# First feed-forward layer in 64-row halves of the array, second layer behind the values (beacon attention and maxout FFN, one core)

## The chip, the cores and the metric

One core of one Trainium2 chip. The metric is the device time of one execution in microseconds (us). The kernel's inputs and its output are f32 in device memory; inside it works in bf16 with f32 accumulation.

## What is computed

Causal attention over 8 batches of 8 heads, 576 tokens of 64 elements each. In front of the keys stand 16 "beacon" keys that every token sees. The 64-element outputs of the 8 heads are laid side by side, which gives a matrix x of 4608 tokens by 512. A feed-forward network follows: three weight matrices of 512 by 768, of whose products the elementwise largest is kept, and an output matrix of 768 by 512.

```
scores = q @ k_all^T / 8, causal on the 576 keys, open on the 16 beacons
a      = exp(scores - max);  a /= sum(a)
x      = heads side by side of (a @ v_all)
h      = maximum(maximum(x @ w1, x @ w2), x @ w3)
out    = h @ w_out
```

## The kernel before

Scores are made transposed, keys on partitions. A pair of heads shares one 128-partition tile: head 0 on partitions 0 to 63, head 1 on 64 to 127, for queries (qT) and keys (kT). So a score matmul contracts over 64 rows, and the two heads' matmuls lie in the two row halves of the array (`emit_scores`, L498 to L521). For each pair there are four groups of such matmuls; each fills at most two PSUM banks, is passed through exp by ScalarE into at_sb (L524) and is then masked, mostly by GpSimd (L543).

`emit_pv` (L563) multiplies the probabilities with the values. Four heads (a "quad", two pairs) run at once in the four 32-column strips of the array; a batch has two quads, each in two halves of 288 queries. A first pass with a matrix of ones gives the sums. `invert_sums` (L598) takes the logarithm and exp(-log) on ScalarE, and `multiply` (L610) scales the results on VectorE into xT, a ring of four batches (L616).

The first layer of the network, `mm1_unit` (L635), uses the full array: for 512 tokens, 128 of the 768 columns and one weight matrix, four matmuls of 128 rows (the four 128-row pieces of the 512 inputs) into one bank, or two such units into two banks. VectorE then copies the bank into hT (first matrix, L654) or takes the maximum with what is there (L656). The first 512 tokens are done in pieces of 256 (`mm1_halves`, L658). The second layer, `mm2_unit` (L677), takes 128 tokens: six matmuls of 512 columns, a copy by VectorE (L694), a store (L720).

Inputs come in f32 by DMA into eight staging buffers (`load_pair`, `load_v`), are cast to bf16, mostly by GpSimd (L255, L311), and are turned, the early pairs by TensorE (L384, L393, L435), those from pair 14 on by a transposing DMA (`cross_piece`, L374). All loads, transposes and stores of the loop go through SP's queue in the order of the steps.

The order of the work on every engine is written out by hand: `first_steps` (to L1072, the first two batches and a part of the network) and `loop_steps` (L1073 to L1614). A step names a function of the table `steps` (L851) and its arguments: "scores" with pair and group, "values" with quad and half, "ffn 1" for one first-layer or second-layer unit, "ffn 2" for two at once, "load", "cast", "cross" and "store" for the movement of data. After the list, `emit_all` (L1616) does the last values and the rest of the network. PSUM has eight banks: two score tiles of two banks (sc), two single banks (pv0, pv1), and one more tile of two banks (wide).

Of the kernel before, what the change touches and what calls it, by code (L numbers as in the profile page):

```python
# [8 lines left out]
FP32 = mybir.dt.float32  # L9
# [7 lines left out]
def kernel(  # L17
# [24 lines left out]
    n_tokb = n_tokens // TOKB  # L42
    FH = d_ff // 2
# [19 lines left out]
    RING = 4  # L63
# [52 lines left out]
    ffn_h = ctx.enter_context(tc.tile_pool(name="ffn_h", bufs=2))  # L116
# [3 lines left out]
    sc_psum = ctx.enter_context(tc.tile_pool(name="sc_psum", bufs=2, space=PSUM))  # L120
    pv_psum = ctx.enter_context(tc.tile_pool(name="pv_psum", bufs=1, space=PSUM))
    ffn_stack = ctx.enter_context(ExitStack())
# [4 lines left out]
    xT = const.tile([128, n_ct, RING * S], BF16, name="xT")  # L127
    NB_PE = Nb * B_PE
# [40 lines left out]
    def single(n=512):  # L169
        i = at_single[0] % 2  # L170
        at_single[0] += 1
        return pv_bank(i, [128, n], FP32)

# [290 lines left out]
    def turn_pair(p, q_copy):  # L464
        ps = next_tile(BF16)
# [32 lines left out]
    def emit_scores(p, gi, idle=0, now=True):  # L498
# [4 lines left out]
        ps = next_tile()  # L503
# [14 lines left out]
        exp = L(emit_exp, p, gi, ps)  # L518
        if now:
            exp()  # L520
        return exp  # L521

    def emit_exp(p, gi, ps):
        nc.scalar.activation(  # L524
            out=both_heads(p, gi), in_=ps[:, :, 0 : g_width(p, gi)], func=AF.Exp, scale=scale
        )
# [34 lines left out]
    ready = [-1]  # L561

    def emit_pv(quad, hf, first=0, last=len(passes), banks=None):  # L563
        b, g = divmod(quad, n_quad)
        v_sb = v_tiles[b]
        for p in range(PPQ * quad, PPQ * (quad + 1)):
            assert all((p, gi) in masked for gi in range(1 if b == 0 and hf == 0 else NG))
# [28 lines left out]
    products = []  # L596

# [12 lines left out]
    def multiply(count=len(passes)):  # L610
        for _ in range(min(count, len(products))):
# [9 lines left out]
            if g == n_quad - 1 and n == len(passes) - 1:  # L621
                ready[0] = 2 * b + hf

    def finish_pv():
        invert_sums()
        multiply()
# [3 lines left out]
    hTs = {}  # L630
    MID = TOKB // 2

    alone = [False]

    def mm1_unit(tb, ft, i, ps):  # L635
        if tb not in hTs:
            hTs[tb] = ffn_h.tile([128, n_ft, TOKB], BF16, name="hT")
        two = len(ps.shape) == 3
        h = hTs[tb][:, ft : ft + 2] if two else hTs[tb][:, ft]
        c0 = tb * TOKB % (RING * S)  # L640
        n0 = min(TOKB, RING * S - c0)
        for f in range(1 + two):
            dst = ps[:, f] if two else ps
            for x0, o0, n in ((c0, 0, n0), (0, n0, TOKB - n0)):
                for ct in range(n_ct if n > 0 else 0):
                    nc.tensor.matmul(  # L646
                        dst[:, o0 : o0 + n],
                        w_in[i][:, ct, 128 * (ft + f) : 128 * (ft + f + 1)],
                        xT[:, ct, x0 : x0 + n],
                        start=(ct == 0),  # L650
                        stop=(ct == n_ct - 1),
                    )
        if i == 0:
            (by_act if alone[0] else by_dve)(h, ps)  # L654
# [3 lines left out]
    def mm1_halves(tb, ft, i, lo, hi, ps):  # L658
        if tb not in hTs:
            hTs[tb] = ffn_h.tile([128, n_ft, TOKB], BF16, name="hT")  # L660
        h = hTs[tb][:, ft : ft + 2, lo:hi]
        ps = ps.rearrange("d (f t) -> d f t", f=2)
        for f in range(2):
            for ct in range(n_ct):
# [3 lines left out]
                    xT[:, ct, tb * TOKB + lo : tb * TOKB + hi],  # L668
# [3 lines left out]
        if i == 0:  # L672
            by_dve(h, ps)
        else:
            nc.vector.tensor_max(h, h, ps)

    def mm2_unit(tb, tt, ps):  # L677
        hT = hTs[tb]
        two = len(ps.shape) == 3
        for t in range(tt, tt + 1 + two):  # L680
            for ft in range(n_ft):
                nc.tensor.matmul(  # L682
                    ps[:, t - tt] if two else ps,
                    hT[:, ft, 128 * t : 128 * (t + 1)],
# [4 lines left out]
        if y_pool:  # L689
            y = y_pool[0].tile([128, 2, d_model], FP32, name="y")  # L690
        else:
            y = early.tile([128, 1, d_model], FP32, name=f"y{len(y_out) % 2}")
        n = 1 + two
        nc.vector.tensor_copy(y[:, 0:n], ps if two else ps[:, None])  # L694
        y_out.append((tb * TOKB + 128 * tt, n, y))

    def mm2_last(tb, tt, cuts):
        hT = hTs[tb]
        c0 = tb * TOKB + 128 * tt
        y = y_pool[0].tile([128, 2, d_model], FP32, name="y")[:, 0]  # L700
        for i in range(len(cuts) - 1):
            lo, hi = cuts[i : i + 2]
            ps = single()[:, 0 : hi - lo]
            for ft in range(n_ft):
                nc.tensor.matmul(
                    ps,
                    hT[:, ft, 128 * tt : 128 * (tt + 1)],
# [5 lines left out]
            nc.sync.dma_start(out[c0 : c0 + 128, lo:hi], y[:, lo:hi])  # L713
# [10 lines left out]

    units = []
    for tb in range(n_tokb):
        need = 2 * ((TOKB * (tb + 1) - 1) // S) + 1
        if tb == 0:  # L730
            for n, lo in ((0, 0), (need, MID)):
                for i in range(3):
                    for ft in range(0, n_ft, 2):
                        units.append((n, mm1_halves, (tb, ft, i, lo, lo + MID)))
        for i in range(0 if tb else 3, 3):
            for ft in range(n_ft):
                units.append((need, mm1_unit, (tb, ft, i)))
        for tt in range(TOKB // 128):
# [931 lines left out]
```

## Time and profile before

| what | value |
|---|---|
| median of three runs | 290.21 us (288.81 to 291.39) |
| span of the profiled execution, first to last instruction | 287.1 us |
| instructions in the span | 8822 |
| mean granted TensorE clock | 0.997 |
| TensorE busy | 278.4 us |
| VectorE busy | 169.7 us |
| ScalarE busy | 143.8 us |
| GpSimd busy | 121.6 us |
| read and written in device memory | 35.13 MB, 9.44 MB |

For the profiled execution only its span is given. The three runs are 1.7 to 4.3 us longer than it.

How to read the lines that follow. In the groups of instructions a row is line, engine, operation, output<-inputs, shapes, xcount | busy us, mean ns of one | idle time before them and what ended it. In a timeline a row is start us, duration us from the first start to the last end of the merged instructions, engine, line, operation, shapes, count. A matmul's duration is a model that includes its way through the array; how fast matmuls follow each other is read from their starts. PE is TensorE, PEld its weight loads, DVE VectorE, ACT ScalarE, POOL GpSimd, SP the queue that issues most DMAs.

### The profile page before, as it was taken

Reading aid. Unit: us, or ns where it says so; the run is one execution under the profiler, and the core shown is the slowest. Engines: PE = TensorE matmul, PEld = TensorE weight load, DVE = VectorE, ACT = ScalarE, POOL = GpSimd, SP = SyncE. Lnnn points to the kernel's source line nnn. Section 1 sums busy time; section 2 is a strip of 40 time slices with the busy share of each in tenths; the row PEclk is TensorE's granted clock in tenths of the full one; section 3 lists DMA queues with packets and bytes.
Section 4 is the critical chain, followed back from the end, with each engine's and each line's share of the span. In section 5 each row is a group of like instructions: output and inputs, shape, how many; then the busy total and the mean of one; then the engine's idle time right before and its main releaser. Section 6 shows DMA issues by size and latency. Waiting matters only on the chain.

```text
span 287.1 us, 8822 instructions
## 1 busy us (share of the span) xinstructions
PE 278.4 (97%) x3706; PEld 160.2 (56%) x3731; DVE 169.7 (59%) x317; ACT 143.8 (50%) x242; POOL 121.6 (42%) x252
## 2 busy tenths in 40 slices
PE   8999999999999999999999999999999999999994
PEld 7656777754646454545456787445544545444442
DVE  2456878766575657465745755567466655373372
ACT  3876676835647564736483268444853452201200
POOL 4562327736484584737376446653633230000000
PEclk9999999999999999999999999999999999999998
DMA  8999998999999987999999989999983003002104
GB/s 154 174 166 209 222 245 158 244 204 211 191 158 159 172 118 134 195 176 184 184 229 191 194 170 221 222 168 177 189 323 123 2 2 148 0 0 107 41 0 147
DMA packets 118231, 45.30 MB, mean 158 GB/s; under 512 B 107312, under 2 KB 112944, under 8 KB 118192
## 3 DMA queue, kind: packets, MB, share of 16 engines
q1 hardware_dynamic: 111984, 39.20, 74.7%
q0 software_dynamic: 5648, 5.21, 11.8%
q8 instruction: 29, 0.48, 0.7%
q10 hardware_dynamic: 560, 0.33, 0.5%
q14 instruction: 10, 0.08, 0.1%
HBM read 35.13 MB, written 9.44 MB: 155 GB/s over the span
## 4 chain that ended last, share of the span: by engine, by line
PE 89%; ACT 3%; DMA 2%; DVE 2%; POOL 1%; issue 1%; ACTq 0%; POOLq 0%
PE pv L646 21%; PE sc L646 15%; PE wide L646 8%; PE pv L682 6%; PE sc L509 6%; PE sc L682 5%; PE wide L682 4%; PE pv L584 4%; PE wide L584 4%; PE sc L584 4%; DMA quad<-in_k_dram 2%; PE wide L509 2%; ACT at_sb L524 2%; PE pv L473 2%; PE sc L665 1%; PE pv L665 1%
## 5 line engine op out<-in xcount | busy, mean ns | idle before, releaser
L524 ACT ACTIVATE at_sb<-sc 128x736 bf16<-128x736 f32 (+5 forms) x95 | 79.4, 868 | 59.2 <-PE sc L509 58.6
L543 POOL TENSOR_SCALAR_AFFINE_SELECT at_sb<-at_sb 128x256 bf16<-128x256 bf16 (+2 forms) x143 | 52.4, 385 | 109.3 <-ACT at_sb L524 101.2
L646 PEld LDWEIGHTS <-w_sb 128*128 128x128 bf16 x648 | 61.1, 98 | 60.7 <-issue 4.9
L646 PE MATMUL pv<-xT,w_sb 128*128 128x512 bf16 (+1 forms) x315 | 65.3, 347 | 0.3
L646 PE MATMUL sc<-xT,w_sb 128*128 128x512 bf16 (+1 forms) x205 | 45.6, 363 | 0.7 <-issue 0.2
L656 DVE TENSOR_TENSOR hT<-hT,pv 128x512 bf16<-128x512 bf16 x48 | 32.4, 686 | 13.2 <-PE pv L646 13.2
L524 ACT ACTIVATE at_sb<-wide 128x736 bf16<-128x736 f32 (+3 forms) x33 | 27.7, 840 | 23.6 <-PE wide L509 23.5
L255 POOL CAST p<-st 96x768 bf16<-96x768 f32 x48 | 38.2, 825 | 0.0
L682 PEld LDWEIGHTS <-hT 128*128 128x128 bf16 x210 | 19.5, 98 | 23.5 <-issue 1.1
L616 DVE TENSOR_TENSOR xT<-pv,recip 128x288 bf16<-128x288 f32 (+2 forms) x48 | 14.2, 351 | 26.4 <-ACT recip L606 26.3
L509 PE MATMUL sc<-qT,kT 64*128 64x288 bf16 (+6 forms) x298 | 27.8, 277 | 1.6 <-DVE kT L443 0.7
L656 DVE TENSOR_TENSOR hT<-hT,sc 128x1024 bf16<-128x1024 bf16 (+1 forms) x19 | 20.8, 1104 | 12.6 <-PE sc L646 12.5
L509 PEld LDWEIGHTS <-kT 64*128 64x128 bf16 x400 | 14.6, 94 | 20.8 <-issue 13.0
L584 PEld LDWEIGHTS <-v_sb 128*32 128x32 bf16 (+1 forms) x1408 | 24.8, 96 | 1.7 <-issue 0.6
L646 PE MATMUL wide<-xT,w_sb 128*128 128x512 bf16 (+1 forms) x110 | 24.5, 364 | 0.1
L682 PE MATMUL pv<-w_out_sb,hT 128*128 128x512 bf16 x83 | 19.9, 380 | 0.1
L311 POOL CAST v_sb<-st 128x1536 bf16<-128x1536 f32 (+2 forms) x21 | 18.4, 897 | 0.0
L654 DVE CAST hT<-pv 128x512 bf16<-128x512 f32 x20 | 13.7, 688 | 5.0 <-PE pv L646 5.0
L682 PE MATMUL sc<-w_out_sb,hT 128*128 128x512 bf16 x68 | 16.3, 380 | 0.2
L665 PEld LDWEIGHTS <-w_sb 128*128 128x128 bf16 x144 | 13.0, 98 | 3.4 <-issue 1.4
L606 ACT ACTIVATE recip<-lnd 128x288 f32<-128x288 f32 x32 | 14.2, 443 | 1.0
L694 DVE COPY y<-pv 128x512 f32<-128x512 f32 x14 | 9.7, 692 | 8.4 <-PE pv L682 8.1
(119 smaller groups left out, 278.8 us busy)
## 6 DMA issues: line engine op xcount, KB each, us to landing
st<-in_q_dram SPq DMA_DIRECT2D x24, 288.0 KB, 5.2
st<-in_k_dram SPq DMA_DIRECT2D x24, 288.0 KB, 6.3
st<-in_v_dram SPq DMA_DIRECT2D x24, 256.0 KB, 5.5
out_dram<-y SPq DMA_DIRECT2D x9, 512.0 KB, 3.8
out_dram<-y SPq DMA_DIRECT2D x17, 256.0 KB, 4.1
w_sb<-in_moe_w_dram POOLq DMA_DIRECT2D x6, 384.0 KB, 8.7
st<-in_v_dram SPq DMA_DIRECT2D x8, 224.0 KB, 4.9
st<-in_v_dram SPq DMA_DIRECT2D x8, 160.0 KB, 4.8
```

What stands on the lines that cost most here:

```text
L255: cast(t16.rearrange("p r h d -> p h r d"), st[0:QP, i * NQ2 : (i + 1) * NQ2].rearrange("p (h r d) -> p h r d", h=2, r=QR),)
L311: cast(v_sb[0:n, t:t1].rearrange("p t h d -> p (t h d)"), st[0:n, (t - t_lo) * H * D : (t1 - t_lo) * H * D],)
L509: nc.tensor.matmul(ps[:, e, off : off + q1 - q0], kT[hs, 128 * t : 128 * t + 128], qT[hs, q0:q1], start=True, stop=True, tile_position=(64 ...
L524: nc.scalar.activation(out=both_heads(p, gi), in_=ps[:, :, 0 : g_width(p, gi)], func=AF.Exp, scale=scale)
L543: nc.gpsimd.affine_select(out=view, in_=view, compare_op=ALU.is_ge, fill=0.0, base=x0, pattern=[[0, 2], [1, hi - lo]], channel_multiplier=-1,)
L584: nc.tensor.matmul(ps[bank][32 * j : 32 * j + 32, lo + q0 - qa : lo + qb - qa], lhsT, at_view(PPQ * quad + j // 2, t, j % 2, q0, qb), star ...
L606: nc.scalar.activation(out=recip, in_=lnd, func=AF.Exp, scale=-1.0)
L616: nc.vector.tensor_mul(xT[:, 2 * g + part - 1, c0 + ca : c0 + cb], ps[bank][:, lo : lo + cb - ca], recip[:, ca:cb],)
L646: nc.tensor.matmul(dst[:, o0 : o0 + n], w_in[i][:, ct, 128 * (ft + f) : 128 * (ft + f + 1)], xT[:, ct, x0 : x0 + n], start=(ct == 0), stop ...
L656: nc.vector.tensor_max(h, h, ps)
L665: nc.tensor.matmul(ps[:, f], w_in[i][:, ct, 128 * (ft + f) : 128 * (ft + f + 1)], xT[:, ct, tb * TOKB + lo : tb * TOKB + hi], start=(ct == 0),
L682: nc.tensor.matmul(ps[:, t - tt] if two else ps, hT[:, ft, 128 * t : 128 * (t + 1)], w_out_sb[:, ft, :], start=(ft == 0), stop=(ft == n_ft ...
```

## The change

`first_steps` stays. From the loop's start on:

- First layer. A unit now takes two blocks of 288 tokens (the first time two of 320) and works in the two 64-row halves of the array, each with a block and a PSUM bank of its own. As a half of the array reads only its own 64 partitions, the other 64 rows of weights and of x are copied across: the weights once (wC, six copies on VectorE, step "cross w"), x for each batch (xC, four copies, nearly all on GpSimd, step "cross x"). A unit is 16 matmuls in eight pairs.
- PSUM. From the loop's start there are four tiles of two banks, and each step names the one it uses ("place").
- Order. Score groups and single units alternate. Each batch's second layer ("out", two tiles of 128 tokens, sometimes one) stands behind the values of the batch's second quad. The last units and the last second-layer tiles are now steps of the list as well.
- Buffers. xT holds three batches instead of four; hT is one ring of 1152 tokens; there are four output buffers instead of nine. Four casts at the loop's start move from GpSimd to ScalarE.

The new functions:

```diff
+    blocks = [(TOKB, (2 * S - TOKB) // 2)] + [(S * b, HALF) for b in range(2, B)]
...
+    def cross_w(i, e, copy):
+        copy(wC[i][own(e)], w_in[i][own(1 - e)])
+
+    def cross_x(k, g, e, copy):
+        t0, n = blocks[k]
+        t0 += e * n
...
+        c0 = t0 % (RING * S)
+        copy(
+            xC[k][own(e), 2 * g : 2 * g + 2, 0:n],
+            xT[own(1 - e), 2 * g : 2 * g + 2, c0 : c0 + n],
+        )
...
+    def mm1_next(place, by_i="dve"):
+        k, i, ft = units.pop(0)
...
+        ps = tile_at(place)[:, :, 0:n]
+        cols = slice(128 * ft, 128 * (ft + 1))
+        for ct in range(n_ct):
+            for w, over in ((w_in[i], False), (wC[i], True)):
+                for e in range(2):
+                    c0 = (t0 + e * n) % (RING * S)
+                    x = xC[k][own(e), ct, 0:n] if over else xT[own(e), ct, c0 : c0 + n]
+                    nc.tensor.matmul(
+                        ps[:, e],
+                        w[own(e), ct, cols],
+                        x,
+                        start=(ct == 0 and not over),
+                        stop=(ct == n_ct - 1 and over),
+                        tile_position=(64 * e, 0),
+                    )
+        c0 = t0 % (2 * S)
+        take(i, hT[:, ft, c0 : c0 + 2 * n].rearrange("d (e t) -> d e t", e=2), ps, by[by_i])
...
+    def mm2_next(n, place):
...
+        y = y_pool[0].tile([128, 2, d_model], FP32, name="y")
+        nc.vector.tensor_copy(y[:, 0:n], ps[:, 0:n])
```

The steps at the loop's start, up to the first unit and a little beyond (the last number of a step that uses PSUM is its place):

```diff
+        ("ffn", "pv", 1),
         ("late",),
...
+        ("cross x", 0, 0, 0, "pool"),
+        ("cross w", 0, 0, "dve"),
+        ("cross w", 0, 1, "dve"),
+        ("scores", 8, 0, 0, 3),
+        ("mask", 8, 0, "pool"),
+        ("scores", 8, 2, 0, 1),
+        ("mask", 8, 2, "pool"),
+        ("values", 3, 0, 0),
+        ("invert",),
+        ("values", 3, 1, 2),
+        ("multiply", 3),
+        ("invert",),
+        ("multiply", 3),
+        ("cross x", 0, 0, 1, "pool"),
+        ("cross x", 0, 1, 0, "pool"),
+        ("cross x", 0, 1, 1, "pool"),
+        ("cast", 10, "act", "act"),
+        ("load", 1),
+        ("cast", 11, "act", "act"),
+        ("load", 1),
+        ("cross w", 1, 0, "dve"),
+        ("out", 2, 3),
+        ("store", 1),
+        ("cross w", 1, 1, "dve"),
+        ("out", 2, 1),
+        ("store", 1),
+        ("pair", 10, "act", 0),
+        ("keys", 10, "act"),
+        ("pair", 11, "act", 2),
+        ("keys", 11, "act"),
+        ("scores", 8, 3, 0, 3),
+        ("mask", 8, 3, "pool"),
+        ("unit", 1),
...
+        ("scores", 8, 1, 0, 0),
         ("mask", 8, 1, "pool"),
...
+        ("unit", 2),
```

The end of a later batch, before and after:

```diff
-        ("values", 11, 0, "pv"),
-        ("invert",),
-        ("exp", 24, 2),
-        ("values", 11, 1, "ring"),
...
-        ("multiply",),
-        ("invert",),
-        ("multiply",),
-        ("ffn 2",),
-        ("cast", 28, "pool", "pool"),
-        ("ffn 1", "pv0"),
-        ("scores", 24, 3, 0),
-        ("scores", 25, 0, 0),
...
+        ("unit", 0),
+        ("values", 11, 0, 3),
+        ("invert",),
+        ("values", 11, 1, 1),
+        ("multiply", 3),
+        ("cross x", 4, 1, 0, "pool"),
+        ("invert",),
+        ("multiply", 3),
+        ("cross x", 4, 1, 1, "pool"),
+        ("cast", 28, "pool", "pool"),
+        ("load", 1),
+        ("out", 2, 2),
+        ("store", 1),
+        ("out", 2, 0),
+        ("store", 1),
+        ("scores", 24, 0, 0, 3),
+        ("mask", 24, 0, "pool"),
+        ("unit", 1),
```

More of the change, by code (lines that the diff above doesn't have):

```diff
@@ L620, in multiply, with take, mm1_halves @@
             )
[L621 to L630, printed above, removed]
[L631 to L652 removed]
+            if n == len(passes) - 1:
+                in_xT.add((quad, hf))
+    MID = TOKB // 2
+    def take(i, h, ps, by_i=None):
         if i == 0:
[L654 removed]
+            (by_i or by_dve)(h, ps)
         else:
             nc.vector.tensor_max(h, h, ps)
[L658 to L661, printed above, removed]
+    def mm1_halves(ft, i, lo, ps):
         ps = ps.rearrange("d (f t) -> d f t", f=2)
```

1078 lines of the change are left out of this document (532 added, 546 removed).

## The prediction

> **What bounds the kernel now.** I read the profile's page first (busy times, then the chain of work that ended last), then the table of stretches, then the timeline of single stretches.
>
> ```profile
> PE 278.4 (97%) x3706; PEld 160.2 (56%) x3731; DVE 169.7 (59%) x317; ACT 143.8 (50%) x242; POOL 121.6 (42%) x252
> PE 89%; ACT 3%; DMA 2%; DVE 2%; POOL 1%; issue 1%; ACTq 0%; POOLq 0%
> ```
> ```profile
> 0.00:55.20 55.20, 51.60 (x966) 38.66 (x967) 35.06 (x104) 37.75 (x62) 27.39 (x68) 1.00 1.08 196
> 55.20:283.40 228.20, 226.70 (x2742) 121.49 (x2766) 134.27 (x213) 106.04 (x180) 94.18 (x185) 1.00 0.84 149
> ```
>
> TensorE (PE) is busy 97% and is 89% of the chain. The second fence gives, for each stretch, its length and the busy time of PE, its weight loads, VectorE (DVE), ScalarE (ACT) and GpSimd (POOL). The changed list of steps begins at 55.2 us. From there to 283.4, PE is busy 226.7 of 228.2 us at granted clock 1.00. No other engine passes 59% of that stretch, so after 55.2 us only a change in PE's own time, or a new wait, can move the end.
>
> A busy PE is not a streaming PE, though. The next rows show where it pays without streaming: start, time from the first start to the last end, shape, count.
>
> ```profile
> 122.05 2.75 PE L682 MATMUL pv<-w_out_sb,hT 128*128 128x512 bf16 x12
> 124.64 1.03 PE L646 MATMUL pv<-xT,w_sb 128*128 128x512 bf16 x4
> ...
> 125.28 0.38 PE L646 MATMUL pv<-xT,w_sb 128*128 128x512 bf16 x1
> 125.60 0.32 PE L509 MATMUL sc<-qT,kT 64*128 64x336 bf16 x2
> ...
> 125.75 0.37 PE L509 MATMUL sc<-qT,kT 64*128 64x288 bf16 x4
> ...
> 125.87 0.25 PE L509 MATMUL sc<-qT,kT 64*128 64x208 bf16 x2
> 125.96 0.32 PE L509 MATMUL wide<-qT,kT 64*128 64x288 bf16 x4
> 126.22 0.39 PE L646 MATMUL pv<-xT,w_sb 128*128 128x512 bf16 x1
> ...
> L646 PEld LDWEIGHTS <-w_sb 128*128 128x128 bf16 x648 | 61.1, 98 | 60.7 <-issue 4.9
> ```
>
> - Full array: 12 matmuls of 512 columns from 122.05 to 124.64, 0.2158 us each (512 columns at 2.4 a ns and 2.5 ns over). The 98 ns weight loads cost nothing.
> - 64-row pairs: the 288-column pair starts at 125.75, the next at 125.87: 0.12 us for both matmuls, again 288/2.4 and some 2.5 ns. The 208-column pair takes 0.09. Two halves run at once, their loads hidden.
> - Turning from one layout to the other costs. The last full matmul before the scores starts at 125.28, the scores at 125.60: 0.32 where 0.216 would do. Back: a 288 and an 80-column pair from 125.96 need 0.155 but the full matmul starts at 126.22, 0.26 later. Each turn is about 0.1 us (0.098 in what follows).
>
> **The change, part by part.**
>
> *Turns.* Scores and first layer now share the 64-row layout; second-layer matmuls (full array) stand together behind the values (32-column). Counting changes of layout along TensorE's instructions in program order gives 141 before and 90 after: 51 x 0.098 = **-5.0 us**, all on the path.
>
> *First layer's streaming.* Before: 504 passes of 512 and 144 of 256 columns at L646, 504 x 0.2158 + 144 x 0.109 = 124.5 us. After: 144 pairs of 320 and 864 of 288 columns, 144 x 0.1358 + 864 x 0.1225 = 125.4. **+0.9 us.** Scores, values, turnings and second layer keep their matmuls. The rows show pairs in chains of five at most, a unit has eight; nothing in the rows grows along a chain, so I take no excess, and keep one as a rival.
>
> *Eviction of a unit*, 128x576 f32 from two banks:
>
> ```profile
> L656 DVE TENSOR_TENSOR hT<-hT,pv 128x512 bf16<-128x512 bf16 x48 | 32.4, 686 | 13.2 <-PE pv L646 13.2
> L656 DVE TENSOR_TENSOR hT<-hT,sc 128x1024 bf16<-128x1024 bf16 x15 | 18.3, 1217 | 12.6 <-PE sc L646 12.5
> L694 DVE COPY y<-sc 128x1024 f32<-128x1024 f32 x5 | 6.1, 1225 | 3.0 <-PE sc L682 3.0
> ```
>
> Between 0.686 and 1.217, by columns 0.75 us, under the unit's 8 x 0.1225 = 0.98. A batch has 18 of them, twelve multiplies and two or three output copies: 13.5 + 4 + 2.8 = 20 us of DVE in some 30 of PE. Hidden; of two alternating places one is free 0.3 us before it is wanted. The same margin for an exp is near nothing where two score groups use one place with a single unit between. I add **0.3 us** for such ties (0 to 1).
>
> *Copies of x* (POOL, 25) *and of the weights* (DVE, 6 of 64x3072). No row of before shows a copy that changes partitions.
>
> ```profile
> L311 POOL CAST v_sb<-st 128x1536 bf16<-128x1536 f32 x7 | 10.3, 1465 | 0.0
> L311 POOL CAST v_sb<-st 80x512 bf16<-80x512 f32 x7 | 4.3, 613 | 0.0
> ...
> L606 ACT ACTIVATE recip<-lnd 128x288 f32<-128x288 f32 x32 | 14.2, 443 | 1.0
> L604 ACT ACTIVATE lnd<-pv 128x288 f32<-128x288 f32 x16 | 6.7, 416 | 6.6 <-PE pv L584 6.6
> ```
> ```profile
> 58.12 0.89 DVE L616 TENSOR_TENSOR xT<-pv,recip 128x288 bf16<-128x288 f32 x3 [1.82 <-ACT recip L606]
> ```
>
> POOL: 0.83 ns a column and 0.19 us, so 0.67 us for 576 columns, 17 us in all. On the path only if the batch's first unit waits: 0.42 + 0.44 + 0.89 + 2 x 0.67 = 3.1 us after the batch's last values, with 5.2 us or more of second layer before that unit. Even at twice the price (4.4) it is covered: **0**. Without that cover each batch would pay the 3 us.
>
> The weight copies have less cover, at the loop's start:
>
> ```profile
> L227 DVE CAST h<-h 96x384 bf16<-96x384 f32 x2 | 0.6, 352 | 3.8 <-DMA h<-in_k_dram 3.8
> ...
> L323 DVE CAST v_sb<-st 80x512 bf16<-80x512 f32 x1 | 0.4, 424 | 0.0
> ```
> ```profile
> 55.02 1.27 DVE L675 TENSOR_TENSOR hT<-hT,pv 128x512 bf16<-128x512 bf16 x2
> ...
> 51.83 0.86 DVE L541 TENSOR_TENSOR at_sb<-at_sb,tri 128x256 bf16<-128x256 bf16 x1
> ```
> ```profile
> L541 DVE TENSOR_TENSOR at_sb<-at_sb,tri 128x224 bf16<-128x224 bf16 x4 | 1.1, 266 | 0.7 <-ACT at_sb L524 0.7
> ```
> ```profile
> 50.95 1.61 POOL L255 CAST p<-st 96x768 bf16<-96x768 f32 x2
> ```
> ```profile
> L459 DVE COPY kT<-sc 128x576 bf16<-128x576 bf16 x4 | 3.0, 749 | 0.9 <-PE sc L393 0.9
> ...
> L448 ACT COPY qT<-sc 128x576 bf16<-128x576 bf16 x3 | 1.9, 639 | 2.8 <-DVE kT L459 2.7
> ...
> L323 ACT CAST v_sb<-st 128x512 bf16<-128x512 f32 x3 | 1.9, 622 | 1.0 <-DVE hT L673 1.0
> ```
>
> The f32 casts grow by 72 ns for 128 columns, 0.56 ns each: 424 + 2560 x 0.56 = 1.86 us is the upper end. Half the bytes a column is the lower, 1.0. I take 1.0, as two-byte sources are all that the copy reads, and keep 1.86 for the range.
>
> The Trainium skill, page "VectorE: DVE Perf Modes", section "The perf-mode tier table", gives 693 ns for a bf16 copy of 2048 elements in SBUF, four a cycle; an estimate from it for 3072 is 0.96 us, and the sum would be the same.
>
> Then the order on DVE from 56.3 us (end of the 55.02 row): two copies to 58.3; the two sets of multiplies to 60.1; a third copy, which I let wait 0.7 us for POOL, because the mask at 51.83 took 0.86 us while POOL cast (the 50.95 row), against 0.27 for a shape only an eighth smaller; to 61.8; output copy to 63.0; fourth copy to 64.0; output copy to 65.25. PE has by then done scores, values, two second-layer pairs (5.2) and two turnings, and wants its first unit's place at 64.5: wait 0.75. Next the kT copies (two of 0.75) and behind each the qT copy (0.64, on ACT) hold the places of the next score group and unit: 0.25 and 0.6. **+1.6 us.** The last two weight copies fall between evictions whose margin is 0.3 us, and meet POOL's casts: **+0.5.**
>
> *DMA.* Attention steps come later against PE time than before: by the steps' PE time after 55.2, scores of pair 16 at 75 instead of 58, of pair 28 at 169 instead of 141. Loads therefore arrive earlier than needed. Only the casts of pairs 11 to 13 move forward (pair 11 from 13.7 to 3.6 after the start).
>
> ```profile
> 46.79 0.42 SPq L202 DMA_DIRECT2D st<-in_q_dram  x1
> 47.26 1.00 SPq L202 DMA_DIRECT2D st<-in_k_dram  x1
> ...
> 62.06 0.45 SPq L202 DMA_DIRECT2D st<-in_k_dram  x1
> ```
> ```profile
> st<-in_k_dram SPq DMA_DIRECT2D x24, 288.0 KB, 6.3
> ...
> out_dram<-y SPq DMA_DIRECT2D x17, 256.0 KB, 4.1
> ```
>
> Pair 11 is issued at 47.3 and lands some 6.3 later, before its cast at 58.8; pair 13 (62.06) lands by 69, cast at 72.7. The stores queue on SP behind loads; with four output buffers, a store of 4 us and at most three a batch of 30 us: 0. The four casts of 96x768 that ACT takes over, each under 0.95 us by its 0.62 for 512 columns, lie under the 5.2 us of second layer: 0. The smaller ring of x (three batches for four) and the two-batch ring of hT are written a batch or more after their last reader: 0.
>
> *Sum:* -5.0 + 0.9 + 0.3 + 1.6 + 0.5 = -1.7 against the profiled 287.1: 285.4. The median run, 290.21, is 3.1 above that span. **Predicted 288.5 us.**
>
> **The rivals.**
>
> 1. *The copies hide.* Fourth copy and POOL do not meet, and no tie shows: -4.1, 286.1. For it: the waits above are each under 0.8 us. Against: DVE, PE and ACT all arrive within a microsecond.
> 2. *The copies are dear.* At 1.86 us, four copies delay DVE by 3.4 us more, the last two by some 1: 288.5 + 3.8 = 292.3, no gain left. For it: no row at that size. Against: half the bytes.
> 3. *Slower: the pairs lose their overlap in long chains.* The place is the unit's eight pairs. The first pair after a turn takes 0.15 us for 336 columns (125.60 to 125.75), 0.011 over its streaming. If every pair paid that: 1008 x 0.011 = +11, 299.6. It decides from (1.7 + 2.9) / 1008 = 4.6 ns a pair, where the time is 1% above before. Against: the second pair (0.12) shows none.
>
> The Trainium skill, page "TensorE: Matmul & The Clock Gate", section "Measured speedup vs the span model", has four row tiles at 3.07 times one, not 4, which speaks for this third case; pairs in this trace do better.
>
> **How the numbers follow.** About 1% is what a measurement of this kernel can tell from no change (its three runs spread 288.8 to 291.4). Chances: forecast 0.45 (its own range 287 to 290.5), copies hide 0.22, copies dear 0.18, lost overlap 0.15. The range reaches to 286.0 and 293.0: it takes in the first two rivals and leaves out the third. Faster by over 1% (below 287.3): 0.22 and a fifth of the forecast's, 0.31. Slower by over 1% (above 293.1): 0.15 and a little of the dear copies, 0.17. Within: 0.52.
>
> **What would show it.** Right: a 288-column pair of the first layer every 0.12 us; some 0.1 us lost at each remaining turn; DVE weight copies near 1 us; PE's idle time after 55.2 us in one cluster between 63 and 72 us. Wrong: pairs over 0.127 us; copies near 2 us; POOL's x copies over 1.4 us with first units waiting for them; waits for evictions in every batch.

## The result, and the profile after

| | before | changed |
|---|---|---|
| median of 20 runs each, same chip | 289.46 us (288.09 to 291.39) | 291.70 us (289.72 to 296.94) |
| profiled execution: time, span | span 287.1 us | 290.32 us, span 288.4 us |
| ratio of the times | | 1.0063, 95% interval 1.0041 to 1.0084 |

Slower by 0.6%, where 0.3% to 0.6% faster was forecast (288.5 against a median of 289.46 to 290.21). The time lies in the range and within 1% of before, but on the other side of it than forecast. The ratio leaves out two runs of the changed kernel, of 295.11 and 296.94 us, that ran in a slower state with a granted clock of 0.988; the medians are of all 20 runs. In a second set of runs the ratio is 1.0039 (1.0017 to 1.0061).

Of the page after, the first lines that answer to those shown of before, then the two stretches, to the loop's start and from there to the last matmul:

```profile
PE 276.4 (96%) x5091; PEld 206.4 (72%) x5099; DVE 183.9 (64%) x336; ACT 154.1 (53%) x247; POOL 138.4 (48%) x274
PE 74%; DMA 6%; POOL 6%; SPq 4%; ACT 4%; issue 3%; DVE 2%; POOLq 0%; ACTq 0%
```
```profile
0.00:55.40 55.40, 51.76 (x967) 38.61 (x969) 35.04 (x104) 37.76 (x62) 27.40 (x68) 1.00 1.08 194
55.40:285.10 229.70, 224.67 (x4127) 167.79 (x4134) 148.50 (x232) 116.30 (x185) 110.96 (x207) 1.00 0.84 148
```

Before, the second stretch had 226.70 us of busy TensorE in 228.20. Now there is less work, 224.67, in a longer stretch, 229.70: idle time in it went from 1.5 to 5.0 us. The saving is there, and new waits have taken more than it. Where they lie is in the list of waits, from 60 us to the last matmul, of the changed kernel (engine, tile, line, what ended the wait: us in all, times, longest):

```profile
PE t L698 <- DVE hT L629: 2.2, 1, 2.2
PE t L698 <- issue: 1.7, 1, 1.7
PE t L698 <- ACT qT L452: 0.3, 1, 0.3
```

Before, this list had one row:

```profile
PE sc L646 <- issue: 0.2, 1, 0.2
```

There are two large stops now. The first, in the timeline around 72 us:

```profile
69.79 0.82 DVE L629 CAST hT<-t 128x640 bf16<-128x640 f32 x1 [0.47 <-PE t L698]
...
70.64 3.21 DVE L668 COPY wC<-w_sb 64x3072 bf16<-64x3072 bf16 x1
...
70.74 1.17 POOL L315 CAST v_sb<-st 128x512 bf16<-128x512 f32 x2
...
72.08 0.34 PE L513 MATMUL t<-qT,kT 64*128 64x288 bf16 x4
...
72.22 2.33 POOL L259 CAST p<-st 96x768 bf16<-96x768 f32 x2
...
73.78 1.54 DVE L629 CAST hT<-t 128x640 bf16<-128x640 f32 x2
...
74.64 0.31 PE L698 MATMUL t<-xT,w_sb 64*128 64x320 bf16 x2 [2.22 <-DVE hT L629]
```

VectorE's fifth weight copy takes 3.21 us, while GpSimd casts. The two evictions queued behind it start at 73.78, and TensorE, out of PSUM places, stands from 72.3 to 74.6. The fourth copy, with no cast beside it, took 0.95 us.

The second stop stands in the middle of a unit, between its fourth pair and its next:

```profile
179.76 0.28 PE L698 MATMUL t<-xT,w_sb 64*128 64x288 bf16 x2
179.88 0.29 PE L698 MATMUL t<-xC,wC 64*128 64x288 bf16 x2
...
181.90 0.30 PE L698 MATMUL t<-xT,w_sb 64*128 64x288 bf16 x2 [1.73 <-issue]
182.02 0.30 PE L698 MATMUL t<-xC,wC 64*128 64x288 bf16 x2
```

The releaser is "issue": TensorE waited for no semaphore. Its operands were long there, since the unit had begun. What it waited for is not in this list; the DMA queues gave the clue. The queue that the page calls "instruction" moved, before, after, and with the full rows of the second experiment:

```profile
q8 instruction: 29, 0.48, 0.7%
```
```profile
q8 instruction: 40, 0.66, 1.0%
```
```profile
q8 instruction: 32, 0.52, 0.8%
```

All its packets have 16,384 bytes. The three traces have 7,465, 10,221 and 8,212 records of TensorE's instructions (matmuls, weight loads and some 30 others, mostly waits for semaphores). In blocks of 256 (64 bytes each) these fill 29.2, 39.9 and 32.1 packets. These packets are TensorE's program. The changed kernel runs through it over a third faster, because a unit of 0.98 us is 32 instructions, where four full-array matmuls of 0.86 us were eight.

So theory F: TensorE stops when it comes to the end of a block before the next one is there. The stop at 179.88 fits. A packet started at 179.0, ran 1.37 us on transfer engines that were full, and TensorE went on 1.5 us after its end. Its rivals: the stop belongs to this place in the work (H), or it is chance.

### The profile page after: what moved, and what is told of

It reads as the page before. It is cut to its first block, busy times and chain, and to the rows that moved or that the text cites. A ratio compares the mean times of both kernels' runs of the same rounds, so it can differ in the third digit from the quotient of the medians.

```text
span 288.4 us, 11666 instructions
## 1 busy us (share of the span) xinstructions
PE 276.4 (96%) x5091; PEld 206.4 (72%) x5099; DVE 183.9 (64%) x336; ACT 154.1 (53%) x247; POOL 138.4 (48%) x274
## 4 chain that ended last, share of the span: by engine, by line
PE 74%; DMA 6%; POOL 6%; SPq 4%; ACT 4%; issue 3%; DVE 2%; POOLq 0%; ACTq 0%
PE t L698 35%; PE t L724 14%; PE t L582 9%; PE t L513 5%; SPq L211 3%; DMA st<-in_q_dram 3%; POOL at_sb L541 3%; DMA quad<-in_k_dram 2%; ACT at_sb L522 2%; PE pv L477 2%; POOL p L259 2%; PE pv L637 2%; PE sc L637 1%; PE sc L513 1%; DVE wC L668 1%
## 5 line engine op out<-in xcount | busy, mean ns | idle before, releaser
L698 PE MATMUL t<-xT,w_sb 64*128 64x288 bf16 (+1 forms) x1008 | 130.2, 285 | 4.3 <-DVE hT L629 2.2
L698 PE MATMUL t<-xC,wC 64*128 64x288 bf16 (+1 forms) x1008 | 130.2, 284 | 0.0
L522 ACT ACTIVATE at_sb<-t 128x992 bf16<-128x992 f32 (+1 forms) x96 | 82.7, 864 | 57.5 <-PE t L513 50.1
L631 DVE TENSOR_TENSOR hT<-hT,t 128x576 bf16<-128x576 bf16 (+1 forms) x84 | 63.6, 763 | 31.2 <-PE t L698 31.2
L698 PEld LDWEIGHTS <-w_sb 64*128 64x128 bf16 x1008 | 53.2, 94 | 15.9 <-issue 5.9
L698 PEld LDWEIGHTS <-wC 64*128 64x128 bf16 x1008 | 52.8, 94 | 10.9
L724 PE MATMUL t<-w_out_sb,hT 128*128 128x512 bf16 x202 | 46.3, 379 | 0.4
L513 PE MATMUL t<-qT,kT 64*128 64x288 bf16 (+4 forms) x288 | 33.4, 279 | 0.1
L522 ACT ACTIVATE at_sb<-sc 128x736 bf16<-128x736 f32 (+5 forms) x28 | 23.1, 861 | 4.3 <-PE sc L513 4.3
L637 PEld LDWEIGHTS <-w_sb 128*128 128x128 bf16 x144 | 13.0, 98 | 3.9 <-issue 1.6
```

The costliest lines, as they stand in the source:

```text
L513: nc.tensor.matmul(ps[:, e, off : off + q1 - q0], kT[hs, 128 * t : 128 * t + 128], qT[hs, q0:q1], start=True, stop=True, tile_position=(64 ...
L522: nc.scalar.activation(out=both_heads(p, gi), in_=ps[:, :, 0 : g_width(p, gi)], func=AF.Exp, scale=scale)
L637: nc.tensor.matmul(ps[:, f], w_in[i][:, ct, 128 * (ft + f) : 128 * (ft + f + 1)], xT[:, ct, lo : lo + MID], start=(ct == 0), stop=(ct == n ...
L698: nc.tensor.matmul(ps[:, e], w[own(e), ct, cols], x, start=(ct == 0 and not over), stop=(ct == n_ct - 1 and over), tile_position=(64 * e, 0),)
L724: nc.tensor.matmul(ps[:, u], h_tile(tt + u, ft), w_out_sb[:, ft, :], start=(ft == 0), stop=(ft == n_ft - 1),)
```

## The experiments

### The casts behind the weight copies; the same order in full rows; more transfers; before again

```diff
 ("cross w", 2, 0, "dve"),
-("cast v", 2, 1, "pool"), ("load", 1),
...
-("cast", 12, "pool", "pool"),
...
 ("cross w", 2, 1, "dve"),
 ("scores", 9, 1, 0, 0), ("mask", 9, 1, "pool"),
+("cast v", 2, 1, "pool"), ("load", 1),
...
+("cast", 12, "pool", "pool"),
```

> The changed kernel with two casts of GpSimd (second piece of the third batch's values, and pair 12) moved behind the sixth weight copy; the copies stay on VectorE, same place, same work. Theory A (VectorE's copy is held up by GpSimd's casts of float32): the fifth weight copy, 3.21 us in the changed kernel, comes down to 0.95 to 1.2 us, since only masks run beside it; the wait of 2.2 us on the eviction at 72 us goes, and the time falls by 2.0 to 2.4 us against the changed kernel (about 289.4 by its median of 291.7). Rival B (VectorE has simply more work between 56 and 79 us than time): the copy may shorten, but the evictions behind it stay late, and a wait of 1 us or more stands within 5 us of the old place; gain under 1 us. The stop of 1.9 us in the middle of a unit near 180 us is not touched by this edit; if it is a matter of when transfers happen to run, it may be there, be elsewhere, or be missing.

Measured: 288.85 us, ratio to before 0.9977 (0.9954 to 1.0000): 2.85 us less than the changed kernel's 291.70, 1.9 less than the 290.73 of its second set of runs. (The cast of pair 13 moved with the two others.) The copies, shortest, middle and longest in ns, and TensorE's waits from 55 us:

```profile
L668 DVE COPY wC<-w_sb x6: 953/956/1039, 56.0 to 73.0; 64x3072 bf16<-64x3072 bf16 x6
```
```profile
PE t L582 <- issue: 1.5, 2, 1.1
PE t L582 <- POOL at_sb L541: 1.0, 2, 0.6
PE t L698 <- issue: 0.3, 2, 0.2
PE t L698 <- ACT qT L452: 0.3, 1, 0.3
```

The same copies in the same queue take 0.95 to 1.04 us once no cast runs beside them, and the wait on the eviction is gone. Theory A holds; VectorE had the time. Part of the gain went into a new wait, the second row: in the values of quad 7 TensorE waits for masks that stand on GpSimd behind the cast of pair 19, and that cast waits for a transposing DMA:

```profile
122.33 1.59 POOL L259 CAST p<-st 96x768 bf16<-96x768 f32 x2 [4.51 <-DMA qT<-p]
123.88 1.73 POOL L541 TENSOR_SCALAR_AFFINE_SELECT at_sb<-at_sb 128x224 bf16<-128x224 bf16 x5
```

TensorE came there some 2.4 us earlier; the transfers did not.

The second kernel undoes the row halves alone (no copies of x or weights, same order of steps, blocks and places):

```diff
-for ct in range(n_ct):
-    for w, over in ((w_in[i], False), (wC[i], True)):
-        for e in range(2):
...
+for e in range(2):
+    c0 = (t0 + e * n) % (RING * S)
+    for ct in range(n_ct):
+        nc.tensor.matmul(ps[:, e], w_in[i][:, ct, cols], xT[:, ct, c0 : c0 + n],
...
```

> The changed kernel's order and its blocks of 288 and 320 tokens, but each first-layer matmul on all 128 rows of the array; no copies of x or weights. Turns of the array's layout by the order of the steps: 214 in the loop against 35 counted the same way. Theory A (a turn costs about 0.1 us, rows in pairs stream as fast as whole rows): 179 more turns by 0.098 = +17.5 us, less what the copies cost at the start (2.4 + about 0.9 us) and less the stop in mid-unit (1.9 us): profiled span about 288.4 + 17.5 - 5.2 = 300.7 us. Theory F (the stop of 1.9 us is TensorE out of instructions: 40 blocks of 16 KB fetched against 29 before): here there are about 1000 matmuls and 1000 weight loads fewer, some 32 blocks, and no stop of over 1 us inside a unit. Rival G (the turns are cheap and the rows in pairs are what costs): time below the changed kernel's, 288 or less.

Measured: 304.03 us, ratio 1.0512 (1.0488 to 1.0536), span 301.9. With the two large stops taken off the changed kernel's span (288.4 - 2.4 - 1.9 = 284.1), the 179 turns cost 17.8 us, 0.099 each. Rival G falls. Its only wait of TensorE after 55 us:

```profile
PE t L695 <- ACT qT L452: 0.3, 1, 0.3
```

No stop in mid-unit. And the small waits at the loop's start, by the starts of matmuls 0.22, 0.24 and 0.49 us in the changed kernel (64.8, 66.2 and 66.7 us), are here 0.22, 0.25 and 0.49, with no copy anywhere: they come from the second layer's output copies and the turned pairs, not from the weight copies.

The third adds transfers where there were nearly none:

```diff
+def load_again(p):
+    load_pair(p)
+    stage.pop(("pair", p))
...
 ("unit", 1),
+("load again", 12),
```

> The changed kernel with 15 loads more (each 576 KB of q and k, read again into the staging ring and used by nobody) in the last two batches, 200 to 262 us, where the transfer engines are nearly idle. Theory F (TensorE waits for its next 16 KB block of instructions, which is late when the transfer engines are full and dense work, the 240 short matmuls and loads of a quad's values, eats up what is left): the blocks fetched after 200 us start later than before, 2 us and more behind instead of under 1 us, and one or more stops of 0.3 to 2 us that wait for no semaphore appear after 200 us, at an instruction count of about 445 behind the last block asked for; time +0.5 to +4 us. Rival H (the stop is the pairs' own, or an accident of the trace): no such stop after 200 us, time within 0.5 us of the changed kernel. Either may have small added waits of the transposes behind the loads on SyncE's queue.

Measured: 290.96 us, ratio 1.0073 (1.0043 to 1.0102), between the changed kernel's two medians; the forecast of +0.5 us or more is not shown. But a stop of 0.55 us that waits for no semaphore appeared at 215.00 us, where neither profile of the changed kernel has one behind 194 us.

Counting TensorE's recorded instructions from the start of the trace shows what the list of waits can't. The stops of over 0.25 us that no semaphore ends (length from one start to the next; turns, some 0.31 us, left out):

| kernel | start us (length us), count |
|---|---|
| changed | 56.25 (0.33), 1985; 179.88 (2.02), 6589 |
| casts later | 55.76 (0.64), 1985; 118.01 (0.43), 4289; 146.49 (1.31), 5313; 180.42 (0.48), 6593 |
| more loads | 56.10 (1.10), 1985; 147.49 (0.35), 5313; 180.46 (1.01), 6593; 192.10 (0.64), 7105; 215.00 (0.55), 7873 |
| full rows | 56.35 (0.30), 1985 |

Every count is 193 more than a multiple of 256, but for 6589. That trace lacks some records (10,221, where a second trace of the same kernel has 10,229, and the stop at 6593). Chance, one in 256 for each, is out.

The packets themselves say it more directly. At a count of 193 + 256 i the block of the queue's i-th packet begins. In the 13 profiles of this case TensorE crosses 399 such counts behind 54 us, and never less than 1.32 us after the end of the i-th packet. All 34 stops of over 0.25 us at these counts (or up to four below, where records are missing) end 1.3 to 1.8 us after it; two more, of 0.31 us, are turns. So a stop ends when its packet has come. The late packet also starts late: the one of the stop at 179.88 started when 183 of the 256 instructions of the block then running were through; behind 225 us, where the transfer engines are nearly idle, the same profile's packets start within 40 instructions of TensorE's crossing into the block ahead of theirs. The added loads delay them: the nine packets from 212 to 265 us start 1.05 us behind that crossing, on average, where the changed kernel's two profiles have -0.15 and 0.01 us.

The kernel before, run beside itself:

> The kernel before, unchanged, beside itself. All theories: a ratio of 1.000, to within 0.002, and this gives the granted clock and the span of each of its runs. Theory K (the changed kernel draws TensorE's clock down more often: 0.988 to 0.994 in 9 of its 20 runs): here at most 2 runs in 20 below 0.999. Rival: the clock is drawn down as often here, and it explains nothing of the difference.

Measured: 289.24 us, ratio 0.9993 (0.9976 to 1.0010). Granted clock at 0.997 or above in all of 12 runs, though under 0.999 in three, more than expected; the changed kernel's was under 0.995 in 8 of its 20. The list of waits has no row.

### Shifting the blocks; a second cast later; copies on GpSimd

```diff
-("out", 2, 3),
+("out", 2, 3, 2),
...
+w = d_model // parts
+for c in range(0, d_model, w):
...
```

> The changed kernel with the second-layer matmuls of the first nine tiles of 128 tokens cut into two of 256 columns: the same columns streamed, 54 matmuls and 54 weight loads more, 48 of these 108 instructions at 58 us and 60 at 95 us. Theory F (TensorE stops when it reaches a boundary of its 256-instruction blocks, at a count of 448 + 256 i, before the block asked for has come): the boundaries come 108 instructions earlier in the work behind 100 us, so the stop between 179 and 183 us is gone, and stops of 0.3 to 1.5 us appear where the boundary now falls behind a quad's values, by the changed kernel's own record of instructions at about 95, 117 and 150 us, at a count of 448 + 256 i again; the wait of 2.2 us at 72 us stays; time within 1 us of the changed kernel. Rival H (the stops belong to a place in the work: a unit behind the values of quad 6, or a transpose issued at that time): the stop stays within 2 us of 180 us. Rival H2 (chance): no stop, or stops at counts that are no multiple of 256 off 448.

Measured: 290.73 us, ratio 1.0048 (1.0027 to 1.0069). The stop near 180 us is gone, and one of 0.91 us stands at 97.29 us, at a count of 3521, 193 over a multiple of 256. That is at one of the three places named; at the second (119.6) the boundary cost under 0.1, at the third nothing. The work at 180 us is the same as ever; only its place in the program moved by 108 instructions. Theory F stands, H falls. The same profile shows a cost that no theory had: the granted clock behind the first stop (length, busy time of PE, weight loads, VectorE, ScalarE, GpSimd, clock, DMA):

```profile
72.00:74.00 2.00, 0.12 (x4) 0.00 (x1) 2.00 (x2) 0.78 (x1) 2.00 (x2) 1.00 0.92 124
74.00:76.00 2.00, 1.66 (x23) 1.31 (x24) 1.97 (x3) 0.00 (x0) 2.00 (x5) 0.91 1.07 230
76.00:78.00 2.00, 2.00 (x18) 1.45 (x16) 1.69 (x3) 0.00 (x0) 1.16 (x1) 0.50 1.34 218
78.00:80.00 2.00, 2.00 (x36) 1.33 (x36) 0.73 (x2) 1.00 (x1) 0.74 (x2) 0.73 1.29 244
```

TensorE stands for 2.3 us, and from 76 to 79 us it runs at half clock, 18 matmuls in 2 us.

Next, the first experiment with the cast of pair 19 and its two transposes behind the masks of pair 15:

```diff
-("cast", 19, "pool", "pool"), ("load", 1),
...
 ("mask", 15, 1, "pool"),
+("cast", 19, "pool", "pool"), ("load", 1), ("cross", 19, 0), ("cross", 19, 1),
```

> The kernel of the first experiment (two casts behind the sixth weight copy), and the cast of pair 19 with its two transposes behind the masks of pair 15: there GpSimd stood 4.5 us waiting for a transpose, five masks waited behind it, and TensorE waited 1.6 us for them in the values of quad 7. Theory: that wait goes, 1.0 to 1.6 us less than the first experiment, median 287.4 to 287.9, ratio to the kernel before 0.992 to 0.995. Rival (the transfers bound the stretch): the wait comes back on a later cast or on the queries and keys of a later pair; gain under 0.5 us.

Measured: 288.03 us, ratio 0.9959 (0.9937 to 0.9980): faster than before and than the changed kernel, but not by all that was expected, and its interval overlaps that of the first experiment. The wait for masks is gone. What is left besides the row for qT are stops without a semaphore, at counts of 1985, 5310 and 6589 (this trace, too, has 10,221 records, eight short):

```profile
PE t L698 <- issue: 2.0, 1, 2.0
PE t L582 <- issue: 1.4, 2, 1.0
```

The other way to free the copies from the casts:

```diff
 ("cross x", 0, 1, 1, "pool"),
+("cross w", 2, 0, "pool"), ("cross w", 2, 1, "pool"),
...
-("cross w", 2, 0, "dve"),
...
-("cross w", 2, 1, "dve"),
```

> The changed kernel with the last two weight copies on GpSimd, behind its x copies at the loop's start where it is idle from 62 to 68 us; the cast of pair 19 later as in the run beside it. Theory A (the fifth copy's cost was VectorE held up by GpSimd's casts): a copy of 64x3072 takes about 3.3 us on GpSimd (64x640 took 0.71), so GpSimd is free again at about 69 us, the wait of 2.2 us at 72 us goes, and masks of the first pairs are 1 to 1.5 us late, which the values at 78 us do not feel: time as the run beside it, within 0.5 us. Rival B: the masks and casts behind are late until 78 us, and TensorE waits 1 us or more in the values of quad 4; time 1 to 2 us above the run beside it.

Measured: 290.35 us, ratio 1.0018 (0.9997 to 1.0040), 2.3 us above the run beside it. Theory A's forecast failed; rival B was nearer in size (1 to 2 us), and had the place wrong:

```profile
62.80 6.16 POOL L668 COPY wC<-w_sb 64x3072 bf16<-64x3072 bf16 x2
63.32 3.04 DVE L668 COPY wC<-w_sb 64x3072 bf16<-64x3072 bf16 x1
66.39 1.22 DVE L732 COPY y<-t 128x1024 f32<-128x1024 f32 x1
...
67.67 0.31 PE L698 MATMUL t<-xT,w_sb 64*128 64x320 bf16 x2 [1.78 <-DVE y L732]
```

Now VectorE's fourth copy runs beside GpSimd's first, and takes 3.04 us for 0.95. So it isn't casts of float32 alone: a long copy on GpSimd does the same.

Last of this group, fewer warming matmuls of the same length in all:

```diff
-("busy", 31, 174),
+("busy", 23, 235),
```

> The run with both casts later, and the first warming matmuls as 23 of 235 columns for 31 of 174: the same columns, 16 instructions fewer ahead of everything, so the boundaries of the instruction blocks come 16 instructions later in the work. Theory F: by the first experiment's record of instructions, with 6 us from request to use, the shortfalls behind the four worst values go from 2.6 to 1.8 us: 0 to 1 us less than the run beside it, and stops, where there are any, at a count of 448 + 256 i. Rival (the stops are set by when the transfers run, not by the count): no difference outside the interval.

Measured: 289.33 us, ratio 0.9993 (0.9969 to 1.0017), 1.3 above the run beside it, not 0 to 1 below; the intervals overlap, so in time the rival is not excluded. The stop near 179 us is gone; the one in the values at 146.07 us grew to 2.14, at a count of 5310 (records are missing here too). The places go by the count; how long a stop is, my shortfalls did not foretell, and no run shows the 6 us from request to use that they were worked out with.

### No idle TensorE; loads behind the values; the changed kernel again

```diff
-("scores", 9, 2, 0, 0),
+("scores", 9, 2, 14, 0),
```

> The changed kernel with 14 spare matmuls of 320 columns (about 1.9 us, on the warming tile, summed into nothing) ahead of the scores that TensorE issues last before the wait of 2.2 us at 72 us, so that it is busy while the fifth weight copy holds the evictions back; the eviction comes when it came. It tells what that stop costs besides its own length: in the run with the shifted boundaries the profile has the granted clock at 0.50 from 76 to 78 us, right behind the stop, and 0.992 to 0.994 over the whole of 7 runs in 12. Theory K (a stop of over 2 us can let the clock drop to half for some 2 to 3 us behind it): here the wait on the eviction is under 0.5 us, no run of the 12 lies under 0.998 in granted clock, and the median is that of the changed kernel's runs at full clock, some 0.5 to 1 us less than the changed kernel beside it. Rival (the clock drops for another reason, the denser rows in pairs among them): runs at 0.992 to 0.994 here too.

Measured: 290.33 us, ratio 1.0020 (1.0006 to 1.0034). No wait on the eviction is left, and no run of 13 has a granted clock under 0.998. (The shifted kernel, on which the expectation leaned, had 8 runs in 12 under 0.995.) The median is 0.4 us under the changed kernel beside it, with intervals that overlap: the clock's share of the median is small, 0.4 us if any. But the eviction did not come when it came before. In this profile the same copy beside the same casts took 1.52 us:

```profile
71.19 1.52 DVE L668 COPY wC<-w_sb 64x3072 bf16<-64x3072 bf16 x1
```

So the run shows TensorE kept busy, and not that the wait would have stood there without the spare matmuls.

```diff
-("cast", 18, "pool", "pool"), ("load", 1),
+("cast", 18, "pool", "pool"),
...
 ("cross", 18, 1),
+("load", 1),
```

The same for pairs 22 and 26.

> The run with both casts later, and of the pairs of loads that stood right ahead of the values of quads 6, 8 and 10 (two loads of q and k, 1.15 MB, issued within 8 us of those values) one moved behind the unit and the transposes that follow the values. Theory F (blocks of instructions come late behind these transfers): the stops at the counts 448 + 256 i near 118, 145 and 179 us shrink from 0.4 to 2 us each to under 0.4; 1 to 2 us less than the run with both casts later (288.0), median 286.0 to 287.0. Rival (the transfer engines are full whichever loads come first): the stops move or stay, gain under 0.5 us; or a late load delays a cast and masks wait behind it.

Measured: 288.52 us, ratio 0.9955 (0.9930 to 0.9981): no gain, and the stop near 178 us is longer, not shorter:

```profile
PE t L698 <- issue: 2.4, 1, 2.4
```

The stop at 145 us is gone. The edit's theory (order these loads otherwise and the blocks come in time) failed; the rival holds.

> The changed kernel, unchanged, beside the runs with edits, on the same chip. All theories: ratio to the kernel before 1.004 to 1.009, the wait of 2.2 us at 72 us there again. Theory F: in its profile stops at counts 448 + 256 i, of 0.3 to 2.5 us, at 56, 118, 146, 180 or 191 us, not all of them, 1 to 3 us in sum. Theory K: some 5 runs in 12 with a granted clock under 0.998, and these 1 to 2 us above the others.

Measured: 290.73 us, ratio 1.0039. The wait of 2.2 us at 71 us is there, stops at counts of 5313, 6593 and 7105 (145.89, 179.01 and 193.59 us; 0.50, 2.29 and 0.87), and 4 runs in 12 under 0.995, which are not clearly slower than the others (290.6 to 292.0 against 289.0 to 291.8). In this profile the half clock stands behind the stop without a semaphore:

```profile
180.00:182.00 2.00, 0.70 (x10) 0.57 (x11) 0.62 (x3) 0.00 (x0) 0.66 (x1) 0.96 1.67 187
182.00:184.00 2.00, 2.00 (x20) 1.48 (x18) 0.75 (x1) 0.73 (x1) 0.41 (x1) 0.50 1.68 98
```

So either stop can do it. It doesn't always: the run with both casts later had a stop of 2.0 us in its profile, and none of its 12 runs lies under 0.998.

## Why the prediction was wrong, point by point

| step | forecast us | measured us |
|---|---|---|
| turns | -5.0 | -5.1 (51 at 0.099, full rows) |
| streaming of the first layer | +0.9 | +0.9 |
| ties | +0.3 | +0.55 (0.27 at 125.8 for a mask; 0.14 at 134.6 and 199.3) |
| x copies | 0 | 0 |
| loop's start | +1.6 | +0.95 |
| last two weight copies | +0.5 | +2.4 |
| stops without a semaphore | none | +1.9 (2.1, before 0.15) |
| sum, to the last matmul | -1.7 | +1.6 (profiles: 285.09 less 283.45, +1.6) |

The table explains the two profiled executions, whose spans differ by 1.3 us; the medians differ by 2.2. The changed kernel's profiled run, 290.32 us, lies 1.4 us under its median, and its second profile, of a run of 291.95 us, has 3.4 us of stops without a semaphore for the 2.1 of the first. The prediction put the median 3.1 us above the span; but each run is only 1.7 to 2.2 us longer than its own span, so the profiled run of before was faster than the median too.

*Turns and streaming: right.* A 288-column pair every 0.12 us, to the end of the chain of eight:

```profile
182.77 0.30 PE L698 MATMUL t<-xT,w_sb 64*128 64x288 bf16 x2
182.90 0.30 PE L698 MATMUL t<-xC,wC 64*128 64x288 bf16 x2
183.02 0.30 PE L698 MATMUL t<-xT,w_sb 64*128 64x288 bf16 x2
183.14 0.30 PE L698 MATMUL t<-xC,wC 64*128 64x288 bf16 x2
183.26 0.30 PE L698 MATMUL t<-xT,w_sb 64*128 64x288 bf16 x2
```

The third rival, lost overlap, is refuted, and with it the use I made of four row tiles at 3.07: two row halves do the work of two here.

*Evictions and x copies: right.*

```profile
L631 DVE TENSOR_TENSOR hT<-hT,t 128x576 bf16<-128x576 bf16 (+1 forms) x84 | 63.6, 763 | 31.2 <-PE t L698 31.2
L679 POOL COPY xC<-xT 64x576 bf16<-64x576 bf16 (+1 forms) x26 | 18.1, 695 | 33.5 <-DVE xT L615 33.3
```

0.75 and 0.67 us were forecast; no unit of a later batch waits for x.

*Loop's start: near in size, wrong in cause.* The price of a weight copy by itself, 1.0 us, was right, so the second rival (1.86) falls. (Its terms, 3.4 and 1 us, add up to 4.4, which would have made it 292.9, not 292.3.) But the same waits stand in the kernel without copies. The first four copies cost nothing that these runs can tell.

*The step that failed: "The last two weight copies fall between evictions whose margin is 0.3 us, and meet POOL's casts: +0.5."* The meeting was seen, its price was not: 3.21 us for one copy, 2.4 us of TensorE's path. I had let the third copy wait 0.7 us for one GpSimd instruction and did not ask how many stand in a row beside the fifth: a cast pair, a mask, a cast pair. The first experiment takes these away and the copy is 0.95 us; the seventh puts a long GpSimd copy beside another and that one takes 3.04. The Trainium skill, page "SBUF — State Buffer", section "SBUF: two separate sides", states that VectorE's fast copies and GpSimd share one pair of ports as an exclusive lock, taken by whichever starts first for its whole instruction, the other standing still. The size agrees: both held-up copies are longer by 2.1 to 2.3 us. So do their ends. The fifth copy ends, at 73.85, 0.81 us after a cast (73.04), and the next cast takes 1.56 us for 0.82:

```profile
72.22 0.82 POOL L259 CAST p<-st 96x768 bf16<-96x768 f32 x1
72.98 1.56 POOL L259 CAST p<-st 96x768 bf16<-96x768 f32 x1
```

The same 0.81 us behind the end of a GpSimd instruction stands in the sixth copy (1.42 us, to 76.77 behind 75.96), in the copy beside GpSimd's (to 66.36 behind 65.55) and in the copy of 1.52 us of the kernel with spare matmuls (to 72.71 behind 71.90). The copy stands while GpSimd works, and GpSimd's next instruction stands while the copy works. What the page's order does not give is how many pass: the fifth copy is recorded 0.1 us ahead of the first cast, while a mask still runs, and three casts and a mask go ahead of it, here and in the three other profiles that have this wait; in the sixth copy and in the one of 1.52 us it is a single cast. Which it will be these runs do not show.

*What the prediction did not have: TensorE's own instructions.* I counted the instructions of each queue that a step is moved past, and never TensorE's, 7,465 to 10,221. In the ten profiles with row pairs the stops at block boundaries behind 54 us (each less 0.12 for the matmul) sum to 1.6 to 4.4 us, 2.8 in the mean; in the three without (before twice, full rows) to 0.5 or less. The list above has 1.9 for the first profile, less than most. Their length differs from profile to profile. The Trainium skill, page "Runtime: NRT & Kernel Launch", section "Instruction fetch mechanics", has the blocks (16 KiB, 256 instructions, fetched by a queue of the sequencer's own), and calls the cost of a boundary mostly hidden. The block size agrees with every count here; the cost was hidden in the kernels with 29 and 32 blocks, and is not with 40.

Shown is that the stops fall on block boundaries, end 1.3 to 1.8 us after the end of a block's packet, move when the program's count moves, and are all but missing with fewer instructions. That transfers make the blocks late is shown for the added loads: packets started some 1.1 us later and a stop appeared behind 200 us, though the time did not follow. Moving three pairs of loads did not help. What else decides a stop's length stays open, as does how much of the 2.8 us fewer transfers would save. A kernel with fewer instructions around the values of those quads was not tried.

## What to carry to other kernels

Price a copy by what runs on the engine that can hold it up, through the whole of its queue and not one instruction of it: a copy of 0.95 us took 1.4 us when one cast passed it and 3.2 when four instructions did. Here two steps moved by a few places were worth 2 to 3 us of a change that was to bring 1.7. Count the instructions of the bounding engine as a resource: a rewrite that does the same streaming in over three times as many instructions a microsecond (32 in 0.98 against 8 in 0.86) can run short of program where dense work follows dense work. And when a bound is relieved, look for the next late thing at each place: the 2.4 us won at 72 us met a transposing DMA at 122.

## What the runs showed of the hardware

- A stop of TensorE of about 2.3 us can be followed by half clock for some 3.4 us: by the three rows of the shifted kernel (0.09 + 0.50 + 0.27) x 2 us / 0.5, and behind 180 us in the changed kernel's second profile (0.04 + 0.50 + 0.31) x 2 / 0.5, where the third row is the next:

```profile
184.00:186.00 2.00, 2.00 (x28) 1.62 (x26) 0.82 (x2) 0.78 (x1) 0.64 (x2) 0.69 0.73 121
```

- Runs with a granted clock under 0.995 came with such stops: 8 of 20, 4 of 12, 8 of 12 and 2 of 5 in the kernels that have the wait at 72 us (changed, again, shifted, more loads), 6 of 12 with the copies on GpSimd and their wait of 1.8 us at 66 us; 0 of 12, 0 of 12 and 0 of 13 in those without it (casts later, both later, TensorE kept busy), 0 of 12 before and 0 of 5 in full rows. The run with fewer warming matmuls had 3 of 12 and the one with the loads behind 3 of 12, without the wait at 72 us but with stops of 2.1 and 2.7 us at a block's end.
- TensorE's program comes in blocks of 256 instructions; idle time at a count of 193 over a multiple of 256, with "issue" as its releaser, was a block that came late. TensorE went on 1.3 to 1.8 us after the end of the block's packet.
- A 64x3072 bf16 copy on VectorE (0.95 us) and GpSimd's casts or copies do not run at once: the copy ended 0.81 us after a GpSimd instruction in each of four cases, and the next GpSimd instruction took 0.6 to 0.7 us longer (3.38 us for 2.75, 1.56 for 0.82).
- The 98 ns weight loads are hidden behind matmuls of 288 columns too: eight of them in full rows take 1.15 us from the first start to the last end, and what full rows cost is the turns.

```profile
180.17 1.15 PE L695 MATMUL t<-xT,w_sb 128*128 128x288 bf16 x8
```
